# A linear-attention and two-MoE kernel: block transposes by DMA in SBUF, zeros in seven parts, routing over four products

## Chip, cores, metric

One core of one Trainium2 chip. The metric is the device time of one execution in microseconds (us), the median of the runs shown.

## What is computed

Three layers in a row, all float32. Cut from the reference:

```python
# attention: batch 8, heads 8, seq 576, head_dim 64
kv  = einsum('bhsd,bhse->bhde', k, v)
out = einsum('bhsd,bhde->bhse', q, kv)
x   = out / sqrt(mean(out*out, -1) + 1e-6) * g_norm      # -> [4608 tokens, 512]
# first MoE layer, dense: d_ff 768
h = maximum(maximum(x @ w1, x @ w2), x @ w3)
x = h @ w_out
# second MoE layer: 8 experts, the best 2 of each token, d_ff 1024
noisy = x @ w_gate + log1p(exp(x @ w_noise)) * noise
out[mask] += top2_w * (maximum(x[mask] @ w1[e], 0) @ w2[e])
```

Each float32 operand of the large products is held as a high and a low part (`hi`, `lo`), and a product is three passes over these: hi*hi, hi*lo, lo*hi.

## The kernel before

The 4,608 tokens are cut into nine chunks of 512 (0 to 8). The program has two halves: the chunks run through attention, the first MoE layer and routing (up to about 702 us), and then units of 128 to 512 tokens run through the experts. Every engine has one queue that it works off in order; the order is that in which the Python program writes the instructions. In chunk 0 a small planner, `run_tasks`, sets that order; the change leaves it alone.

**One chunk c.** The loop at the end of `body` writes for g = 0 to 17 first `misc1(c, g)` and then `g1(c, g)`, and after the 18 products `window(c)`. A product `g1` (line 311 for the matmuls) is 12 matmuls of 128x512 into one of four `hbank` PSUM banks; `g1_top` (lines 327 and 329, "top") takes it to `hm`, on ScalarE for every third product and on VectorE for the others, and after each third product `hsplit` (lines 315 and 319) writes a slice f of `hT` as hi and lo. Chunk 1 is shorter: half of its tokens were done in chunk 0, so its products have 256 columns.

**The window.** `g2(c, i, f0, f1)` (line 357) multiplies the six slices of `hT` of 128 tokens, block i, with `w_out`: 36 matmuls into two of the four `abank` banks. When a block is complete, lines 360 to 365 copy it out, half on VectorE and half on ScalarE, to `RA`. The last slice, f = 5, comes out of product 17.

**Attention for chunk c+1 runs inside chunk c.** At g = 10 `kv_pair` (line 192) and `kv_out` make the key-value product. `ao` (line 214) is 64 small matmuls for half the chunk; `norm` squares them (ScalarE, line 231), sums (VectorE, line 235), makes the inverse root with a few small instructions (lines 239 to 247) and scales (VectorE, line 251) into four buffers `xn`, one per block of 512 columns. Half 0 of `ao` stands at g = 14, half 1 in the window after block 1. Then `xtrans` turns the result for the next chunk's products: four transposes by TensorE into a PSUM bank (line 273), ScalarE writes `xT` hi (line 277) and VectorE lo (line 282). Four `xtrans` per window: two after block 1, two inside block 3. Product 0 of chunk c+1 reads all of `xT`.

**Loads.** SyncE's queue (SP) loads for each chunk the noise (16 KB), q into `RB`, and k, v into `KV0` and two buffers of `STG`; these stand at g = 0 and start when their buffers come free. At g = 11 of chunk 8 it starts the first expert weights (line 144), and then `load_rows` (line 755), a DMA that transposes 16-bit planes from HBM.

**Routing of chunk c-1 runs inside chunk c**: `route_a` (lines 385 to 408) as one block at g = 1, with two loads of the function table of ScalarE; `route_b` at g = 10 (7 in chunk 1), then four row scatters on GpSimd (POOL, line 427), and four more at g = 14 (12 in chunk 1).

**Zeros.** The output is added to later, so it is zeroed first: `zero_out`, one DMA of 9,472 KB from POOL's queue at g = 2 of chunk 2 (line 540).

Of the kernel before, what the change touches and what calls it, by code (L numbers as in the profile page):

```python
# [22 lines left out]
DUMMY = NE * R  # L23
# [62 lines left out]
def body(tc, A, dbg=None):  # L86
# [37 lines left out]
    def hbank():  # L124
        cnt["h"] += 1
        return HB[(cnt["h"] - 1) % 4]

    def abank():
        cnt["a"] += 1
        return AC[(cnt["a"] - 1) % 4]  # L130
# [72 lines left out]
    def ao(c, j, banks):  # L203
        for h in range(2):
            ao_bank[c, 2 * j + h] = banks[h]
        for i in range(2):
            t0 = (2 * j + i) * 128
            for p in range(4):
                o = slice(i * 256 + p * 64, i * 256 + (p + 1) * 64)
                for x in range(2):  # L210
                    t = t0 + x * 64
                    kb = KB[(c * CT + t) // S % 2]
                    for h in range(2):
                        PE.matmul(banks[h][HALF[x], o], qv(c)[HALF[h], p, t:t + 64],  # L214
                                  kb[HALF[h], p * 64:(p + 1) * 64], start=True, stop=True)
# [39 lines left out]
    def norm(c, i, x=None):  # L255
        norm_a(c, i, x)
        norm_b1(c, i, i + 1)
        norm_b2(c, i, i + 1)
        norm_c(c, i)
# [25 lines left out]
    def xtrans(c, i):  # L285
        t = xtrans_pe(c, i)
        xtrans_hi(i, t)
        xtrans_lo(i, t)


    def split(src, w):
        ACT.activation(w[:, 0:1024], src, AF.Copy)  # L292
        DVE.tensor_tensor(w[:, 1024:2048], src, w[:, 0:1024].bitcast(F), op=OP.subtract)  # L293
# [54 lines left out]
    def g2(c, i, f0, f1):  # L348
        if f0 == 0:
            x2b[i] = abank(), abank()  # L350
        s = slice(i * 128, (i + 1) * 128)
        for f in range(f0, f1):
            h = hTf(f)
            w = wo(f // 2)[:, :, f % 2]
            for n, (a, b) in enumerate(((0, 0), (0, 1), (1, 0))):
                for z, (lo, hi) in enumerate(((0, 256), (256, 528))):
                    PE.matmul(x2b[i][z][:, 0:hi - lo], h[:, a, s], w[:, b, lo:hi],  # L357
                              start=f == 0 and n == 0, stop=f == 5 and n == 2)
        if f1 == 6:
            DVE.tensor_copy(lgs[:, i, :], x2b[i][1][:, 256:272])  # L360
            for z in range(2):
                b = x2b[i][z].bitcast(U16).rearrange("p (n t) -> p n t", t=2)
                for q in range(2):
                    (ACT.copy if q else DVE.tensor_copy)(  # L364
                        planes[:, i, q * 512 + z * 256:q * 512 + z * 256 + 256], b[:, 0:256, q])
# [18 lines left out]
    def route_a(c):  # L384
        ACT.activation(nl, lgs[:, :, 8:16], AF.Exp)
        ACT.preload_act_table_set("natural_log")
        ACT.activation(nl, nl, AF.Ln, bias=1.0)
        ACT.preload_act_table_set(LNEXP)
        DVE.tensor_tensor(nl, nl, noise[c % 2], op=OP.mult)
        DVE.tensor_tensor(nl, nl, lgs[:, :, 0:8], op=OP.add)  # L390
        for i in range(4):
            DVE.max(m8[:, i, :], nl[:, i, :])
            DVE.max_index(ix[:, i, :], m8[:, i, :], nl[:, i, :])
        DVE.tensor_copy(ixf, ix[:, :, 0:2])
        for k in range(2):
            DVE.tensor_tensor(oh[:, k], C("iota8").unsqueeze(1).to_broadcast([128, 4, 8]),
                              ixf[:, :, k:k + 1].to_broadcast([128, 4, 8]), op=OP.is_equal)
        DVE.tensor_tensor(Mb, oh[:, 0], oh[:, 1], op=OP.add)
        DVE.tensor_copy(Cb[:, 1, :], Mb[:, 0, :])
        for i in range(1, 4):  # L400
            DVE.tensor_tensor(Cb[:, i + 1, :], Cb[:, i, :], Mb[:, i, :], op=OP.add)
        DVE.tensor_tensor(wt[:, 0, :], m8[:, :, 1], m8[:, :, 0], op=OP.subtract)
        ACT.activation(wt[:, 1, :], wt[:, 0, :], AF.Exp)
        DVE.tensor_scalar(wt[:, 0, :], wt[:, 1, :], 1.0, 1e-9, op0=OP.add, op1=OP.add)
        DVE.reciprocal(wt[:, 0, :], wt[:, 0, :])
        DVE.tensor_tensor(wt[:, 2, :], wt[:, 1, :], wt[:, 0, :], op=OP.mult)
        DVE.tensor_copy(rows[:, :, 512], wt[:, 0, :])
        DVE.tensor_copy(rows[:, :, 513], C("tok", 4 * c, 4 * c + 4))
# [24 lines left out]
    def scatter(c, k):  # L433
        if k == 1:
            DVE.tensor_copy(rows[:, :, 512], wt[:, 2, :])
        for i in range(4):
            scatter_to(si[c % 2][:, 4 * k + i:4 * k + i + 1], rows[:, i, :])
# [98 lines left out]
        POOL.memset(pad, 0.0)  # L536
        DVE.tensor_copy(pad[:, 513:514], C("trash"))

    def zero_out():
        z = POOL.dma_start(A["out"].rearrange("(a p) f -> p a f", p=128),  # L540
                           pad[:, 0:512].unsqueeze(1).to_broadcast([128, OUT_ROWS // 128, 512]))
        zeroed.append(z.ins)
        POOL.dma_start(Xg[DUMMY:DUMMY + 512, :].rearrange("(a p) w -> p a w", p=128),
                       pad.bitcast(U16).unsqueeze(1).to_broadcast([128, 4, 2 * XW]))

    for j in range(2):
        ao(0, j, [abank(), abank()])
# [279 lines left out]
            state["load"] += 1  # L827


    def misc1(c, g):  # L830
        if c == 1 and g == 0:
            POOL.memset(STG[2][64:128, 0:1024], 0.0)
            fills()
        if c == 1 and (g == 0 or 8 < g < 14):
            f = max(g - 8, 0)
            hsplit(f, early(f), 0, 256)
        if c == 2 and g == 2:
            zero_out()
        if g == 0:
            SP.dma_start(noise[c % 2], A["noise"][c])  # L840
        if g == 0 and 0 < c < NCH - 1:
            load_q(c + 1)
            if c + 1 < NB:
                for i in range(3):
                    load_kv(c + 1, i)
        if c > 0:
            if g == 1:
                route_a(c - 1)
            if g == (7 if c == 1 else 10):
                route_b(c - 1)  # L850
                scatter(c - 1, 0)
            if g == (12 if c == 1 else 14):
                scatter(c - 1, 1)
        if 0 < c < NB - 1 and g == 10:
            bank = abank()
            for p in range(4):
                kv_pair(c + 1, p, bank)
            kv_out(c + 1, bank)
        if 0 < c < NCH - 1 and g == 14:
            ao(c + 1, 0, [abank(), abank()])  # L860
            for i in range(2):
                norm(c + 1, i)
        if c == NCH - 1:
            if g == 11:
                spec_pick()
                load_regs(0, spi[0:1, 0:1], spi[0:1, 1:2])
                regE[1] = regE[0]
                regS[1] = SP.value_load(spi[0:1, 2:3], min_val=0, max_val=DUMMY)
                for p in range(3):
                    load_pair(p)  # L870
            if g == 12:
                load_rows(0)
            if g in (13, 14, 15, 16, 17):
                splits(1)

    def window(c):
        nx = c + 1 < NCH

        def fill(i):
            if nx:  # L880
                if i == 0:
                    ao(c + 1, 1, [hbank(), hbank()])
                norm(c + 1, i + 2)

        def trans(i):
            xtrans(c + 1, i)

        if c == 0:
            for i in (2, 3):
                g2(0, i, 0, 3)  # L890
                trans(i)
                g2(0, i, 3, 6)
            xn_n[0] = 0
            return
        for i in range(4):
            g2(c, i, 0, 3)
            if nx and i == 3:
                trans(2)
                trans(3)
            g2(c, i, 3, 6)  # L900
            if nx and i == 1:
                trans(0)
                trans(1)
                fill(0)
                fill(1)
            if not nx:
                if i < 2:
                    for r in range(3 * i, 3 * i + 3 - i):
                        utrans(0, r, 4)
                if i == 1:  # L910
                    load_rows(1)
                splits(1)
# [241 lines left out]
            G2(*fifo.pop(0)[1:])  # L1154

    def table():
        route_a(c)
        yield
        route_b(c)
        scatter(c, 0)  # L1160
        pads()
        yield
        yield from tab_counts()
        yield
        for n, _ in enumerate(tab_build()):
            if n == 2:
                scatter(c, 1)
            yield
        yield
        tab_out()  # L1170
        yield
        for uu in range(2, 4):
            regs_of(uu)
        load_rows(2)
        loads()
# [85 lines left out]
```

## Time and profile before

| | |
|---|---|
| median of 3 runs | 1540.65 us (1538.05 to 1541.68) |
| the profiled execution | 1540.13 us |
| its span, first to last instruction | 1538.4 us |
| TensorE busy | 1508.5 us (98%), mean granted clock 0.994 |
| VectorE, ScalarE, POOL busy | 789.7 us (51%), 644.8 us (42%), 222.3 us (14%) |
| chunks | 1 to 8 begin at about 143.1, 195.6, 269.4, 343.1, 416.9, 490.7, 564.4 and 635.6 us |

Durations below come from the profiled execution. "Busy" counts an instruction from its start to its modelled end; matmuls overlap their neighbours, so the price of a group on TensorE is the distance between starts, not the busy time. In the views by line and in the timelines, a bracket or a last column says how long the engine stood idle before an instruction and which instruction released it. In the views by stretch the last three numbers are the granted TensorE clock, the busy share of the 16 DMA engines and the GB/s that they moved. "To landing" is the time from the issue of a DMA until its data has arrived.

### The profile page before, as it was taken

How to read it: one execution, taken by the hardware profiler on the slowest of the kernel's cores; microseconds unless marked ns; L12 is line 12 of the kernel's file. 1: busy time of each engine (PE TensorE's matmuls, PEld its weight loads, DVE VectorE, ACT ScalarE, POOL GpSimd, SP SyncE). 2: the span in 40 equal slices, each digit the busy share in tenths (PEclk: the TensorE clock that was granted, in tenths of full speed). 3: DMA queues.
4: the chain of work that ended last, by engine and by line, in shares of the span. 5: the costliest groups of instructions: out<-in, count | busy, mean ns of one | idle time of the engine just before them, and what ended most of it. 6: DMA issues, size and time to landing. Idle time of an engine off the chain costs nothing.

```text
span 1538.4 us, 23747 instructions
## 1 busy us (share of the span) xinstructions
PE 1508.5 (98%) x9564; PEld 1304.2 (85%) x9564; DVE 789.7 (51%) x1567; ACT 644.8 (42%) x1042; POOL 222.3 (14%) x326
## 2 busy tenths in 40 slices
PE   5999999999999999999999999999999999999997
PEld 4789989898989898988888888888888888888886
DVE  5985534343435353447454465565364554545543
ACT  3554222222313131335254455556465454645543
POOL 0000211111110202023311102102011011211112
PEclk8999999999999999999999999999999999999999
DMA  8322652030303101063685578778486674957654
GB/s 296 137 83 91 235 220 117 30 117 29 118 36 112 54 32 56 1 192 98 192 208 135 140 210 193 191 225 213 135 210 147 181 196 133 227 128 211 157 151 78
DMA packets 132292, 219.82 MB, mean 143 GB/s; under 512 B 96464, under 2 KB 96720, under 8 KB 114640
## 3 DMA queue, kind: packets, MB, share of 16 engines
q1 hardware_dynamic: 112320, 166.50, 34.2%
q0 software_dynamic: 19856, 51.73, 14.9%
q8 instruction: 77, 1.26, 0.3%
q14 instruction: 39, 0.32, 0.1%
HBM read 146.30 MB, written 51.72 MB: 129 GB/s over the span
## 4 chain that ended last, share of the span: by engine, by line
PE 96%; DMA 1%; DVE 1%; ACT 1%; issue 0%; POOL 0%; SPq 0%; POOLq 0%; DVEq 0%; ACTq 0%
PE bank L311 28%; PE bank L1136 27%; PE bank L1074 26%; PE bank L357 10%; PE bank L192 1%; PE bank L1088 1%; PE bank L214 1%; PE bank L273 1%; DMA pad<-kvr 1%; DMA G<-kv 0%; DMA G<-w1s 0%; PE bank L501 0%; DVE RA L478 0%; DVE B L282 0%; PE bank L493 0%
## 5 line engine op out<-in xcount | busy, mean ns | idle before, releaser
L311 PE MATMUL bank<-B,W 128*128 128x512 f32 (+1 forms) x2160 | 455.4, 371 | 6.7 <-ACT W L482 4.1
L311 PEld LDWEIGHTS bank<-B,W 128*128 128x128 f32 x2160 | 377.4, 190 | 76.0 <-ACT W L482 4.9
L1136 PE MATMUL bank<-W,B 128*128 128x512 f32 x1728 | 421.3, 390 | 0.0
L1136 PEld LDWEIGHTS bank<-W,B 128*128 128x128 f32 x1728 | 320.2, 188 | 63.4
L1074 PE MATMUL bank<-B,W 128*128 128x512 f32 (+1 forms) x1728 | 353.0, 342 | 0.0
L1074 PEld LDWEIGHTS bank<-B,W 128*128 128x128 f32 x1728 | 280.5, 189 | 42.5
L293 DVE TENSOR_TENSOR W<-G,W 128x1024 fp32r<-128x1024 f32 x200 | 242.4, 1224 | 124.5 <-ACT W L292 124.1
L1078 ACT ACTIVATE B<-bank 128x512 fp32r<-128x512 f32 (+1 forms) x176 | 91.5, 520 | 340.8 <-PE bank L1074 340.8
L1079 DVE SCALAR_TENSOR_TENSOR B<-bank,B 128x512 fp32r<-128x512 f32 (+1 forms) x176 | 104.3, 593 | 238.9 <-ACT B L1078 237.9
L292 ACT ACTIVATE W<-G 128x1024 fp32r<-128x1024 f32 x200 | 208.4, 1053 | 39.3 <-PE bank L1136 24.8
L357 PE MATMUL bank<-W,B 128*128 128x256 f32 (+1 forms) x1296 | 163.9, 285 | 0.0
L357 PEld LDWEIGHTS bank<-W,B 128*128 128x128 f32 x1296 | 160.2, 188 | 1.1
L427 POOL DMA_INDIRECT Xg<-RA,si x72 | 72.5, 1007 | 519.4 <-issue 377.5
L329 DVE TENSOR_TENSOR hm<-hm,bank 128x512 f32<-128x512 f32 (+1 forms) x106 | 69.5, 655 | 132.5 <-PE bank L311 125.7
L315 ACT ACTIVATE B<-hm 128x512 fp32r<-128x512 f32 (+1 forms) x53 | 32.1, 606 | 184.2 <-DVE hm L329 184.2
L1074 PE MATMUL bank<-xlo,W 128*128 128x512 f32 x384 | 102.6, 389 | 0.0
L1110 POOL DMA_INDIRECT out<-xn,idt x37 | 61.6, 1664 | 271.6 <-ACT xn L1141 264.6
L1074 PEld LDWEIGHTS bank<-xlo,W 128*128 128x128 f32 x384 | 72.1, 188 | 15.0
L1110 POOL DMA_INDIRECT out<-x2T,idt x19 | 30.4, 1598 | 260.3 <-ACT x2T L1141 257.9
L364 ACT COPY RA<-bank 128x256 uint16<-128x256 uint16 x72 | 25.7, 373 | 87.9 <-DVE RA L364 72.6
L327 ACT ACTIVATE hm<-bank 128x512 f32<-128x512 f32 (+1 forms) x53 | 30.4, 573 | 53.8 <-PE bank L311 41.5
L1110 POOL DMA_INDIRECT out<-hm,idt x19 | 33.0, 1735 | 134.2 <-ACT hm L1141 130.4
(184 smaller groups left out, 1029.7 us busy)
## 6 DMA issues: line engine op xcount, KB each, us to landing
G<-mw SPq DMA_DIRECT2D x100, 1024.0 KB, 5.2
G<-w1s SPq DMA_DIRECT2D x12, 1024.0 KB, 5.1
out<-pad POOLq DMA_DIRECT2D x1, 9472.0 KB
kv<-kv SPq DMA_DIRECT2D x8, 1024.0 KB, 8.0
G<-kv SPq DMA_DIRECT2D x8, 1024.0 KB, 10.0
RB<-qT SPq DMA_DIRECT2D x8, 1024.0 KB, 4.9
G<-kvr SPq DMA_DIRECT2D x7, 256.0 KB, 10.8
Xg<-RA,si POOLq DMA_INDIRECT x72, 2.8
```

The costliest lines, as they stand in the source:

```text
L292: ACT.activation(w[:, 0:1024], src, AF.Copy)
L293: DVE.tensor_tensor(w[:, 1024:2048], src, w[:, 0:1024].bitcast(F), op=OP.subtract)
L311: PE.matmul(bank[:, 0:t1 - t0], w_in(g)[:, a, k, s], x[b][:, k, t0:t1], start=n == 0 and k == 0, stop=n == 2 and k == 3)
L315: ACT.activation(hTf(f)[:, 0, t0:t1], hm, AF.Copy)
L329: DVE.tensor_tensor(hm, hm, bank, op=OP.max)
L357: PE.matmul(x2b[i][z][:, 0:hi - lo], h[:, a, s], w[:, b, lo:hi], start=f == 0 and n == 0, stop=f == 5 and n == 2)
L427: i = POOL.indirect_dma_start(out=Xg, out_offset=bass.IndirectOffsetOnAxis(ap=idx, axis=0), in_=src, in_offset=None)
L1074: PE.matmul(bank[:, 0:n], w[:, a, k, s], x[b][:, k, 0:n], start=z == 0, stop=z == 11)
L1078: ACT.activation(h[:, 0, 0:n], bank[:, 0:n], AF.Relu)
L1079: DVE.scalar_tensor_tensor(h[:, 1, 0:n], bank[:, 0:n], 0.0, h[:, 0, 0:n].bitcast(F), op0=OP.max, op1=OP.subtract)
L1110: d = POOL.indirect_dma_start(out=A["out"], out_offset=bass.IndirectOffsetOnAxis(ap=idt[u % 3][:, i:i + 1], axis=0), in_=y, in_offset=None ...
L1136: PE.matmul(obank[i], h[:, a, s], w[:, b, ff % 2, :], start=ff == 0 and n == 0, stop=ff == 7 and n == 2)
```

## The change

- **Attention (chunks 2 to 8).** Both halves of `ao` stand at g = 12, squares and sums at g = 12 and 13, the inverse roots of all four blocks together at g = 13, the scaling at g = 14 and 15. `planes_out` copies each scaled block as two 16-bit planes (one copy on VectorE, one on ScalarE) into `KV0`; `planes_turn` is one DMA transpose on SP's queue for each two blocks, from `KV0` to `RB`, 128 x 2048 elements of 16 bits (512 KB). In the window, after blocks 0 and 1, `planes_in` merges the planes of two blocks each in an `STG` buffer (again one copy on each engine) and writes `xT` hi and lo from there. TensorE's transposes of these chunks are gone; those of chunks 0 and 1 stay. The blocks of `g2` stand one behind the other.
- **Zeros.** Seven DMAs of 1,280 or 1,536 KB, one at g = 10 of each of chunks 2 to 8, behind the first four scatters.
- **Routing.** `route_a` becomes a generator with three stops; its pieces stand at g = 1, 2, 3 and 4.

```diff
+    def xplanes(c):
+        return [t.bitcast(U16)[:, 0:4096] for t in (KV0, RB)]
+
+    def planes_out(c, b):
+        d = xplanes(c)[0].rearrange("p (b z k i e) -> p b z i k e", b=4, z=2, k=2, i=2)
+        x = xn_of[c, b].bitcast(U16).rearrange("p (i k e z) -> p z i k e", i=2, k=2, z=2)
+        for z in range(2):
+            (ACT.copy if z else DVE.tensor_copy)(d[:, b, z], x[:, z])
+
+    def planes_turn(c, j):
+        src, dst = xplanes(c)
+        SP.dma_start_transpose(out=dst[:, j * 2048:(j + 1) * 2048].rearrange("p (q t) -> p q t", q=16),
+                               in_=src[:, j * 2048:(j + 1) * 2048])
+
+    def planes_in(c, b):
+        p = xplanes(c)[1].rearrange("p (b z n) -> p b z n", b=4, z=2)
+        m = STG[c % 2][:, b * 512:(b + 1) * 512]
+        h = m.bitcast(U16).rearrange("p (n z) -> p n z", z=2)
+        for z in range(2):
+            (ACT.copy if z else DVE.tensor_copy)(h[:, :, z], p[:, b, z])
+        j, k = divmod(b, 2)
+        m = m.rearrange("p (k t) -> p k t", k=2)
+        hi, lo = (x[:, 2 * k:2 * k + 2, j * 256:j * 256 + 256] for x in xT)
+        ACT.activation(hi, m, AF.Copy, scale=gn[:, 0:1])
+        DVE.scalar_tensor_tensor(lo, m, gn[:, 0:1], hi.bitcast(F), op0=OP.mult, op1=OP.subtract)
+
+    def attend(c, n):
+        if n == 0:
+            for j in range(2):
+                ao(c, j, [abank(), abank()])
+        if n < 2:
+            for b in (2 * n, 2 * n + 1):
+                norm_a(c, b)
+        if n == 1:
+            norm_b1(c, 0, 4)
+            norm_b2(c, 0, 4)
+        if n in (2, 3):
+            j = n - 2
+            for b in (2 * j, 2 * j + 1):
+                norm_c(c, b)
+                planes_out(c, b)
+            planes_turn(c, j)
...
-    def zero_out():
-        z = POOL.dma_start(A["out"].rearrange("(a p) f -> p a f", p=128),
-                           pad[:, 0:512].unsqueeze(1).to_broadcast([128, OUT_ROWS // 128, 512]))
+    ZB = [0, 6, 12, 17, 22, 27, 32, 37]
+
+    def zero_out(n):
+        a, b = ZB[n], ZB[n + 1]
+        z = POOL.dma_start(A["out"][a * 128:b * 128, :].rearrange("(a p) f -> p a f", p=128),
+                           pad[:, 0:512].unsqueeze(1).to_broadcast([128, b - a, 512]))
...
-        if c == 2 and g == 2:
-            zero_out()
...
-                route_a(c - 1)
+                ra[c] = route_a(c - 1)
+            if 0 < g < 5:
+                next(ra[c], None)
             if g == (7 if c == 1 else 10):
                 route_b(c - 1)
                 scatter(c - 1, 0)
+                if c > 1:
+                    zero_out(c - 2)
...
-        if 0 < c < NCH - 1 and g == 14:
-            ao(c + 1, 0, [abank(), abank()])
-            for i in range(2):
-                norm(c + 1, i)
+        if 0 < c < NCH - 1 and g >= 12:
+            attend(c + 1, g - 12)
...
         for i in range(4):
-            g2(c, i, 0, 3)
-            if nx and i == 3:
-                trans(2)
-                trans(3)
-            g2(c, i, 3, 6)
-            if nx and i == 1:
-                trans(0)
-                trans(1)
-                fill(0)
-                fill(1)
-            if not nx:
-                if i < 2:
+            g2(c, i, 0, 6)
+            if i < 2:
+                if nx:
+                    for b in (2 * i, 2 * i + 1):
+                        planes_in(c + 1, b)
```

**Where instructions move.** SP's queue between the loads that stand in chunk 1 and those of chunk 2, as a piece of the difference (kv is `KV0`, G an `STG` buffer):

```order
 L163 DMA G_84<-kvr 64x1024
-L840 DMA noise_101<-noise 128x32
+L302 DMA_TRANSPOSE RB<-kv_92 128x16x128 x2
+L890 DMA noise_101<-noise 128x32
 L172 DMA RB<-qT 128x2048
 L155 DMA kv_92<-kv 128x2048
```

The two transposes stand ahead of the next chunk's noise, q and key-value loads; they read the buffer that the key-value load fills and write the one that the q load fills.

VectorE's queue before, in chunk 1, from the scaling of block 0 to the tops of products 16 and 17 (`xn` the scaled blocks, `stat` the sums, line 329 a top, line 319 a low half of `hT`):

```order
L251 TENSOR_TENSOR xn_93<-bank_111,stat 128x512
L235 TENSOR_REDUCE stat<-xn_94 128x8
L239 TENSOR_SCALAR stat<-stat 128x8
L245 TENSOR_TENSOR stat<-stat 128x8
L246 SCALAR_TENSOR_TENSOR stat<-stat 128x8
L247 SCALAR_TENSOR_TENSOR stat<-stat 128x8
L251 TENSOR_TENSOR xn_94<-bank_112,stat 128x512
L329 TENSOR_TENSOR hm_96<-hm_96,bank_105 128x256
L319 TENSOR_TENSOR B_87<-hm_96,B_87 128x256
L329 TENSOR_TENSOR hm_96<-hm_96,bank_107 128x256
L329 TENSOR_TENSOR hm_96<-hm_96,bank_108 128x256
```

The same place in the changed kernel, from the top of product 13 to that of product 16 (line 372 is the top, line 362 the low half of `hT`, line 298 `planes_out`):

```order
L372 TENSOR_TENSOR hm_96<-hm_96,bank_108 128x256
L251 TENSOR_TENSOR xn_93<-bank_111,stat 128x512
L298 COPY kv_92<-xn_93 128x2x2x128
L251 TENSOR_TENSOR xn_94<-bank_112,stat 128x512
L298 COPY kv_92<-xn_94 128x2x2x128
L372 TENSOR_TENSOR hm_96<-hm_96,bank_105 128x256
L362 TENSOR_TENSOR B_87<-hm_96,B_87 128x256
L251 TENSOR_TENSOR xn_95<-bank_109,stat 128x512
L298 COPY kv_92<-xn_95 128x2x2x128
L251 TENSOR_TENSOR x2T_97<-bank_110,stat 128x512
L298 COPY kv_92<-x2T_97 128x2x2x128
L372 TENSOR_TENSOR hm_96<-hm_96,bank_107 128x256
```

Before, blocks 0 and 1 stand ahead of the tops of products 14, 16 and 17 and blocks 2 and 3 in the window; now all four blocks, with a copy of each, stand between the tops of products 13 and 16, ahead of the last slice of `hT`.

## Rows read from the trace of the kernel before

**Rows 1.** The page, parts 1 (busy us, share, instructions) and 4 (chain)

```profile
PE 1508.5 (98%) x9564; PEld 1304.2 (85%) x9564; DVE 789.7 (51%) x1567; ACT 644.8 (42%) x1042; POOL 222.3 (14%) x326
...
PE 96%; DMA 1%; DVE 1%; ACT 1%; issue 0%; POOL 0%; SPq 0%; POOLq 0%; DVEq 0%; ACTq 0%
```

**Rows 2.** Waits of TensorE, whole span: us in total, times, longest us

```profile
PE bank L311 <- DVE hm L329: 1.4, 1, 1.4
```

**Rows 3.** Busy time by stretch: the windows of chunks 1, 7 and 8

```profile
core 0: us, PE busy (x) PEld busy (x) DVE busy (x) ACT busy (x) POOL busy (x), PEclk, DMA share, GB/s
174.72:195.42 20.70, 20.70 (x226) 20.37 (x225) 11.81 (x32) 7.51 (x19) 0.81 (x2) 1.00 1.02 391
...
614.70:635.40 20.70, 20.70 (x225) 20.35 (x224) 10.31 (x27) 6.93 (x17) 0.00 (x0) 1.00 0.01 2
684.55:702.11 17.56, 17.56 (x145) 17.56 (x144) 11.69 (x25) 8.77 (x16) 0.64 (x2) 1.00 0.53 155
```

**Rows 4.** Timeline of TensorE, chunk 2's window: start us, us, what, count

```profile
248.49 8.95 PE L357 MATMUL bank<-W,B 128*128 128x256 f32 x72
257.28 1.03 PE L273 MATMUL bank<-cst,xn 128*128 128x128 f32 x8
258.24 1.16 PE L214 MATMUL bank<-kvt,RB 64*64 64x64 f32 x64
259.33 6.87 PE L357 MATMUL bank<-W,B 128*128 128x256 f32 x54
266.04 0.38 PE L273 MATMUL bank<-cst,xn 128*128 128x128 f32 x2
...
266.91 2.44 PE L357 MATMUL bank<-W,B 128*128 128x256 f32 x18
269.19 3.13 PE L311 MATMUL bank<-B,W 128*128 128x512 f32 x13
```

**Rows 5.** Chain that ended last, products 0 to 9 of chunk 2: start us, us

```profile
195.58 27.22 PE bank L311 x120
```

**Rows 6.** Groups of VectorE, 195 to 700 us: busy us, mean ns, idle before

```profile
L329 DVE TENSOR_TENSOR hm<-hm,bank 128x512 f32<-128x512 f32 x84 | 57.6, 686 | 125.4 <-PE bank L311 120.0 <-ACT hm L327 4.3 <-DVE hm L329 0.5
...
L251 DVE TENSOR_TENSOR xn<-bank,stat 128x512 f32<-128x512 f32 x18 | 12.4, 692 | 1.9
L235 DVE TENSOR_REDUCE stat<-xn 128x8 f32<-128x512 f32 x18 | 12.2, 678 | 5.4 <-ACT xn L231 5.4
```

**Rows 7.** Groups of ScalarE, same stretch

```profile
L315 ACT ACTIVATE B<-hm 128x512 fp32r<-128x512 f32 x42 | 26.5, 632 | 171.4 <-DVE hm L329 171.4
...
L231 ACT ACTIVATE xn<-bank 128x512 f32<-128x512 f32 x18 | 10.7, 597 | 19.4 <-PE bank L214 19.4
```

**Rows 8.** Instructions of line 788: duration ns min/median/max

```profile
L788 DVE COPY mg<-RB x59: 441/452/573, 689.9 to 1512.6; 128x512 uint16<-128x512 uint16 x59
L788 ACT COPY mg<-RB x47: 762/771/788, 690.3 to 1511.2; 128x512 uint16<-128x512 uint16 x47
```

**Rows 9.** Line 755, DMA transposes from HBM

```profile
DMA to landing us min/median/max: 4.2/5.6/16.0
```

**Rows 10.** DMA issues, 698 to 704 us: KB each, us to landing

```profile
RB<-Xg SPq DMA_TRANSPOSE x1, 5.9
```

**Rows 11.** Timeline of TensorE, chunk 1, product 5

```profile
151.82 3.13 PE L311 MATMUL bank<-B,W 128*128 128x256 f32 x24 [1.38 <-DVE hm L329]
```

**Rows 12.** Timeline of VectorE, chunk 1, tops of half width

```profile
151.35 0.94 DVE L329 TENSOR_TENSOR hm<-hm,bank 128x256 f32<-128x256 f32 x2
```

**Rows 13.** Timeline of ScalarE, chunk 8, products 14 to 17 and window

```profile
675.23 2.01 ACT L292 ACTIVATE W<-G 128x1024 fp32r<-128x1024 f32 x2 [3.49 <-DMA G<-mw]
...
686.62 0.63 ACT L315 ACTIVATE B<-hm 128x512 fp32r<-128x512 f32 x1 [2.68 <-DVE hm L329]
```

**Rows 14.** Timeline of SP's queue, chunk 8, product 11

```profile
670.24 1.50 SPq L144 DMA_DIRECT2D G<-mw  x3
```

**Rows 15.** Busy time by stretch while the zeros go out

```profile
177.00:193.00 16.00, 16.00 (x187) 15.67 (x186) 8.87 (x26) 5.33 (x15) 0.00 (x0) 1.00 1.02 385
```

More of the change, by code (lines that the diff above doesn't have):

```diff
@@ L390, in route_a @@
         DVE.tensor_tensor(nl, nl, lgs[:, :, 0:8], op=OP.add)
+        yield
         for i in range(4):
@@ L393, in route_a @@
             DVE.max_index(ix[:, i, :], m8[:, i, :], nl[:, i, :])
+        yield
         DVE.tensor_copy(ixf, ix[:, :, 0:2])
@@ L401, in route_a @@
             DVE.tensor_tensor(Cb[:, i + 1, :], Cb[:, i, :], Mb[:, i, :], op=OP.add)
+        yield
         DVE.tensor_tensor(wt[:, 0, :], m8[:, :, 1], m8[:, :, 0], op=OP.subtract)
@@ L537, in fills @@
         DVE.tensor_copy(pad[:, 513:514], C("trash"))
-    def zero_out():
-        z = POOL.dma_start(A["out"].rearrange("(a p) f -> p a f", p=128),
-                           pad[:, 0:512].unsqueeze(1).to_broadcast([128, OUT_ROWS // 128, 512]))
+    ZB = [0, 6, 12, 17, 22, 27, 32, 37]
[3 more added lines that the diff above has]
+                           pad[:, 0:512].unsqueeze(1).to_broadcast([128, b - a, 512]))
         zeroed.append(z.ins)
-        POOL.dma_start(Xg[DUMMY:DUMMY + 512, :].rearrange("(a p) w -> p a w", p=128),
-                       pad.bitcast(U16).unsqueeze(1).to_broadcast([128, 4, 2 * XW]))
+        if n == 0:
+            POOL.dma_start(Xg[DUMMY:DUMMY + 512, :].rearrange("(a p) w -> p a w", p=128),
+                           pad.bitcast(U16).unsqueeze(1).to_broadcast([128, 4, 2 * XW]))
     for j in range(2):
@@ L827, in loads @@
             state["load"] += 1
+    ra = {}
     def misc1(c, g):
@@ L877, in window @@
         nx = c + 1 < NCH
[L879 to L886, printed above, removed]
         if c == 0:
@@ L890, in window @@
                 g2(0, i, 0, 3)
-                trans(i)
+                xtrans(1, i)
                 g2(0, i, 3, 6)
@@ L895, in window @@
         for i in range(4):
-            g2(c, i, 0, 3)
-            if nx and i == 3:
-                trans(2)
-                trans(3)
-            g2(c, i, 3, 6)
-            if nx and i == 1:
-                trans(0)
-                trans(1)
-                fill(0)
-                fill(1)
-            if not nx:
-                if i < 2:
+            g2(c, i, 0, 6)
[3 more added lines that the diff above has]
+                        planes_in(c + 1, b)
+                else:
                     for r in range(3 * i, 3 * i + 3 - i):
                         utrans(0, r, 4)
+            if not nx:
                 if i == 1:
@@ L1156, in table @@
     def table():
-        route_a(c)
+        for _ in route_a(c):
+            pass
         yield
```

## The prediction

> **What bounds the kernel.** I read the page first: TensorE is busy 98% of the span and holds 96% of the chain that ended last [rows 1]. A kernel of this kind gets shorter only where work leaves TensorE's queue or where TensorE waits. Then its waits: from chunk 1 on there is one, 1.4 us for a top on VectorE [rows 2]; it stands ahead of products 5 and 6 of chunk 1 [rows 11]. Everything else on VectorE, ScalarE, POOL and the DMA queues is hidden today. So the questions are what leaves TensorE's queue, and what comes out from under its cover.
>
> **What leaves TensorE.** The window of chunk 8 shows a window without attention: 144 matmuls in 17.56 us, 4.39 us a block. The windows of chunks 1 to 7 take 20.70 us, the first as the seventh [rows 3]. In these stand 16 transposes and one half of `ao`. The half of `ao` moves to g = 12 and is paid there: it goes from 258.24 to 259.33, 1.09 us [rows 4]. What is left is 20.70 - 17.56 - 1.09 = 2.05 us a window. The transposes alone, from start to start, are 258.24 - 257.28 = 0.96 and 266.91 - 266.04 = 0.87, together 1.83 us [rows 4]; the other 0.2 us is spent around the switches between transposes and matmuls. Seven windows: 7 x 2.05 = **14.3 us**, at least 7 x 1.83 = 12.8. I take 14.3, since the changed window is that of chunk 8, back to back.
>
> **The routing.** In chunk 1 the whole of `route_a` stands ahead of the top of product 1 on VectorE, and product 5 needs that bank. Now only its first piece does; the others come after later tops, and the half-width tops are short, 0.94 us for two [rows 12]. The wait of 1.38 us [rows 11] goes: **-1.4 us**, between 0 (the third and fourth piece hold up product 8 as long) and 1.4. In later chunks products take 27.22 / 10 = 2.72 us [rows 5] and no wait is there to be saved.
>
> **What VectorE and ScalarE take on.** Each block now passes two more copies on each engine. Such a 16-bit copy of 128x512 takes 0.45 us on VectorE and 0.77 on ScalarE [rows 8]; eight a chunk are 3.6 and 6.2 us, against a cover of some 74 us a chunk (269.4 - 195.6), and over the span these engines are busy 51% and 42% [rows 1]. Only two places are tight. In chunks 2 to 7: with `ao` at time 0, product 12 starts at 2 x 1.09 = 2.2, the window at 2.2 + 6 x 2.72 = 18.5, and its blocks end every 4.39 us, the last at 36.1. Product 13 ends at 7.6; its top (0.69), two scalings at 0.69, two copies at 0.45 on VectorE and the last copy on ScalarE (0.77) [rows 6, 8] put the first DMA transpose at about 12, the second, behind the top and split of product 14, at about 16.5. The last slice of `hT` follows product 17 as before. No wait.
>
> In **chunk 1** the products are half as long. From the first square (0.60 us [rows 7], done at 1.09 + 0.60 = 1.7) VectorE has four sums (0.68), four scalings (0.69), four copies (0.45), some 1.2 us of small instructions and eight half-width ones (0.47) [rows 6, 8, 12]: 12.2 us, some 1.3 more in waits for ScalarE, so the last slice of `hT` comes at about 15. The six products last 6 x 1.48 = 8.9 (3.13 us for two [rows 11], less the overlap), so the window begins at 11.1 and asks for slice 5 after 30 matmuls of 4.39 / 36, at 14.8. I charge **+0.5 us**, between 0 and 1.6.
>
> **The DMA transposes.** No row shows one within SBUF. The nearest are those from HBM of 1 MB, twice the bytes: 5.9 us to landing with the queues nearly empty [rows 10], 4.2 the shortest of all and 16.0 the longest, which was beside weights [rows 9]. A half-size one costs between 2.1 (half the shortest) and 16.0; I take 5, near the lone one. Who waits: `planes_in` reads the first after block 0 of the window and its copy-out, at about 24, the second at about 28.3, 12 us after each issue; and product 0 of the next chunk needs `xT` at 36.1, while the two blocks behind 28.3 take about 4 us (copy 0.77, high part 0.63, low part 0.69 as for like shapes [rows 6 to 8], twice). If each takes X and the second queues behind the first, all is ready at 12 + 2X + 4, in time for X up to 10 us. So 5 is hidden, and half of the slowest row (8) is too: **0 us**. Behind these DMAs in SP's queue stand the noise, q and key-value loads of the next chunk but one; they wait for the buffers `RB` and `KV0`, free about 4 us ahead of the window's end, and are asked for at g = 10 or later, 27 us into the next chunk: 0.
>
> The Trainium skill speaks against this step: its page "VectorE: DVE Perf Modes", section "The three transpose paths", gives 1309 ns for one 128x128 transpose by DMA against 390 on TensorE, and the rules below it prefer TensorE where PSUM will do as the target. By that figure, as an estimate, 16 of them one after the other would be 21 us, past the 10 above. Against it speaks the trace's lone megabyte, 32 such squares in 5.9 us [rows 10].
>
> **The zeros.** The one large DMA moved 385 GB/s and kept the DMA engines full [rows 15], and TensorE did not wait; in chunks 2 to 7 nothing is won or lost. The seventh part is new at a bad place. In chunk 8 it goes out just ahead of the first expert weights (SP issues them at 670.24 [rows 14]), 1,280 KB at 385 GB/s, 3.4 us. ScalarE there already idles 3.49 us for these weights [rows 13], its queue carries the splits of the weights and the last slice of `hT`: 686.62 + 0.63 = 687.25 for its high part, which block 0 asks for at 684.55 + 30 x 0.122 = 688.2. So only 1 us of slack; weights late by 1 to 3.4 us cost 0 to 2.5. Both queues share the engines, so I take 2 late, **+0.9 us**.
>
> **The sum** against the profiled execution's own 1540.13 us (span 1538.4 and 1.73 around it; the median of the runs is 0.5 above): 1540.1 - 14.3 - 1.4 + 0.5 + 0.9 = **1525.8 us**, 0.9% faster. A measurement of this kernel tells about 0.2%, 3.1 us, from no change.
>
> **Rivals.**
> - *VectorE and the weights come out from under the cover.* Chunk 1 pays 1.6, chunk 8 pays 2.5, the routing saves nothing and a window saves only 1.83: 1540.1 - 12.8 + 1.6 + 2.5 = 1531.4. For it speaks the small slack at both places; against it that all four at once are needed.
> - *The DMA transposes come late: slower.* Place: product 0 of each of chunks 2 to 8 waits for `xT`. Price: 2 us a chunk for each us of X above 10, so 14 us in all. At X = 11 the gain is used up; at 12 the time is 1525.8 + 28 = 1554, at the 16.0 of the slowest row 1525.8 + 84 = 1610. For it: a source in SBUF is unpriced, and the scatters of g = 14 share the DMA engines. Against it: the lone row, at half of which X is 3.
> - *The 16 squares of one DMA transpose go one after the other*, so that X is beyond the slowest row and the time over 1610. Against it: no row of a transpose is that slow. The figure of the Trainium skill's page named above would make this X = 21.
> - *Nothing changes for TensorE*: the windows keep their length because the 0.2 us and the transposes were filling time in which the tops were awaited. Then 1540. Against it: the window of chunk 8, with more on VectorE (11.69 us against 10.31), is short [rows 3].
>
> **Chances.** The forecast, 1524 to 1529: 0.74. First rival, 1529 to 1534: 0.13. DMA transposes late: 0.08, of which 0.02 still faster, 0.02 within 0.2% and 0.04 slower. One square after the other: 0.03, slower. No effect: 0.02, the same. So faster 0.89, same 0.04, slower 0.07. The range 1523.8 to 1533.5 goes from all costs at zero (1540.1 - 14.3 - 1.4 = 1524.4, less a little) over the first rival, and leaves out late transposes.
>
> **What would show it.** Right: windows of 17.6 us in chunks 1 to 7, TensorE's chain without line 273 after chunk 1, no wait ahead of product 5 of chunk 1, DMA transposes landing in 4 to 8 us. Wrong: waits of product 0 for VectorE's `xT` behind `planes_in`, or of block 0 of the windows of chunks 1 and 8 for ScalarE's half of slice 5, over 2 us.

## The result and the profile after

| | before | changed |
|---|---|---|
| median | 1539.97 us (4 runs, 1538.05 to 1541.68) | 1526.62 us (4 runs, 1525.79 to 1527.96) |
| the profiled execution | 1540.13 us | 1526.44 us |
| its span | 1538.4 us | 1524.7 us |

The ratio is 0.9912, with a 95% interval of 0.9897 to 0.9927: 13.4 us less, where the forecast was 1525.8 us. The page of the changed kernel, with busy time (parts as in [rows 1]), the chain, and TensorE's group of the window (line 400 is `g2` there; its last column is the idle time before it):

```profile
PE 1495.7 (98%) x9452; PEld 1294.1 (85%) x9452; DVE 796.4 (52%) x1539; ACT 675.5 (44%) x1056; POOL 229.0 (15%) x332
...
PE 95%; DMA 2%; ACT 1%; DVE 1%; issue 0%; POOL 0%; SPq 0%; POOLq 0%; DVEq 0%
...
L400 PE MATMUL bank<-W,B 128*128 128x256 f32 (+1 forms) x1296 | 162.1, 286 | 2.1 <-ACT B L358 2.1
```

TensorE has 112 matmuls and 12.8 us of work less; VectorE has 6.7 us more, ScalarE 30.7. In the last row is something new: 2.1 us in which TensorE waits for line 358, the high part of a slice of `hT`. The timeline of TensorE, for chunk 1, chunk 2 and the end of chunk 8:

```profile
142.61 10.22 PE L354 MATMUL bank<-B,W 128*128 128x256 f32 x84
...
191.10 27.37 PE L354 MATMUL bank<-B,W 128*128 128x512 f32 x120
...
226.61 2.10 PE L214 MATMUL bank<-kvt,RB 64*64 64x64 f32 x128
228.64 16.62 PE L354 MATMUL bank<-B,W 128*128 128x512 f32 x72
...
666.96 3.82 PE L400 MATMUL bank<-W,B 128*128 128x256 f32 x30
672.84 15.70 PE L400 MATMUL bank<-W,B 128*128 128x256 f32 x114 [2.06 <-ACT B L358]
688.37 6.98 PE L1111 MATMUL bank<-B,W 128*128 128x512 f32 x30
```

The first row is products 0 to 6 of chunk 1 without a gap, so the wait of [rows 11] is gone. In chunk 2 both halves of `ao` stand together and take 2.03 us (226.61 to 228.64); no row of line 273 is left there. In chunk 8 the new wait of 2.06 us stands at slice 5 of block 0. Busy time by stretch: the windows of chunks 1 and 7 (against 20.70 in [rows 3]), and three stretches behind the wait of chunk 8:

```profile
173.53:191.10 17.57, 17.57 (x146) 17.57 (x145) 10.78 (x26) 9.91 (x19) 0.00 (x0) 1.00 0.36 88
600.27:617.84 17.57, 17.57 (x146) 17.56 (x144) 8.22 (x19) 8.40 (x15) 0.00 (x0) 1.00 0.07 15
...
672.84:676.00 3.16, 3.16 (x14) 3.16 (x15) 2.07 (x6) 0.87 (x3) 0.00 (x0) 0.51 1.05 393
676.00:677.00 1.00, 1.00 (x9) 1.00 (x8) 0.23 (x1) 1.00 (x2) 0.00 (x0) 0.85 0.70 295
677.00:690.00 13.00, 13.00 (x103) 12.71 (x102) 8.44 (x17) 7.89 (x14) 0.00 (x0) 1.00 0.40 85
```

The windows are as short as that of chunk 8 before. Behind the wait the granted clock (third number from the end) is 0.51, its lower level of 1.2 GHz, for some 3 us, and then 1.00 again: 14 matmuls in 3.16 us, where 26 would go at full clock. The window of chunk 8 lasts 688.37 - 666.96 = 21.41 us in place of 17.56: 2.06 of wait and 1.8 at the lower clock.

**The account**, span against span, in us: a chunk lasts 262.66 - 191.10 = 71.56 (the window of chunk 2 is 245.09 to 262.66) and lasted 73.77, and 7 x 2.2 = **-15.4**; the wait in chunk 1 **-1.4**; chunk 8 **+3.8**; chunk 1 began 0.5 earlier, which is in chunk 0, where nothing was changed (over the thirteen profiled executions used here its start scatters between 142.2 and 145.7 us, though no edit touches chunk 0); 0.2 is left over. Together -13.7, from 1538.4 to 1524.7.

Why chunk 8 waits is read on two queues. POOL and SP there, issues with their time (line 589 is a zeros part, line 144 the first expert weights), from the two timelines:

```profile
651.84 0.92 POOL L589 DMA_DIRECT2D out<-pad  x1
...
652.71 2.18 SPq L144 DMA_DIRECT2D G<-mw  x3
```

The same place on ScalarE (line 335 splits weights, line 358 is the high part of the last slice):

```profile
660.76 2.01 ACT L335 ACTIVATE W<-G 128x1024 fp32r<-128x1024 f32 x2 [6.61 <-DMA G<-mw]
...
672.15 0.63 ACT L358 ACTIVATE B<-hm 128x512 fp32r<-128x512 f32 x1 [2.67 <-DVE hm L372]
```

The part is issued 0.87 us ahead of the weights, and ScalarE waits 6.61 us for these, against 3.49 in [rows 13]. Its queue then runs 3.1 us later up to the last slice, which TensorE wants. So the step is the predicted one, and its price four times the predicted one.

The transposes themselves, the 14 of line 302, with the time to landing of the 11 whose landing the trace has:

```profile
L302 SPq DMA_TRANSPOSE RB<-kv x14: 1317/1676/4445, 173.7 to 598.0; - x14
...
DMA to landing us min/median/max: 3.7/3.8/7.9
```

No engine waited for one.

### The profile page after: what moved, and what is told of

Read it like the earlier page. It is cut to its first block, busy times and chain, and to the rows that moved or that the text cites. A ratio compares the mean times of both kernels' runs of the same rounds, so it can differ in the third digit from the quotient of the medians.

```text
span 1524.7 us, 23555 instructions
## 1 busy us (share of the span) xinstructions
PE 1495.7 (98%) x9452; PEld 1294.1 (85%) x9452; DVE 796.4 (52%) x1539; ACT 675.5 (44%) x1056; POOL 229.0 (15%) x332
## 4 chain that ended last, share of the span: by engine, by line
PE 95%; DMA 2%; ACT 1%; DVE 1%; issue 0%; POOL 0%; SPq 0%; POOLq 0%; DVEq 0%
PE bank L354 28%; PE bank L1173 27%; PE bank L1111 26%; PE bank L400 10%; PE bank L192 1%; PE bank L1125 1%; PE bank L214 1%; DMA pad<-kvr 1%; DMA G<-mw 1%; DMA G<-kv 0%; PE bank L547 0%; DVE hm L372 0%; ACT B L277 0%; PE bank L539 0%; ACT W L335 0%
```

## The experiments

The theory after the result: the transposes by DMA save 2.2 us a chunk and are hidden; the routing saves its wait; the seventh zeros part alone costs 3 to 5 us in chunk 8. The rivals: the wait in chunk 8 has another cause; the saving is something else than the transposes; the transposes are close to coming late.

The runs were made on three chips of different speed. The kernel before took 1547.5 us on the chip of the first run of six parts and of the routing, the zeros and the transposes alone; 1547.6 us on that of the changed kernel again, six parts again and the repeated transposes; and 1540.7 us on that of the small and large last part and the one zeros DMA earlier. So each run is compared with the kernel before, or with another kernel, on its own chip.

### Six zeros parts, none in chunk 8

```diff
-    ZB = [0, 6, 12, 17, 22, 27, 32, 37]
+    ZB = [0, 7, 13, 19, 25, 31, 37]
...
-                if c > 1:
+                if 1 < c < NCH - 1:
                     zero_out(c - 2)
```

> The changed kernel with the zeros in six parts, in chunks 2 to 7, none in chunk 8. Theory (the part in chunk 8 makes the first expert weights late, and with them the last slice of hT): TensorE's wait of 2.06 us in block 0 of chunk 8's window goes, the granted clock stays at 1.00 there, chunk 8 shrinks from 70.5 us back to about 66.7, and the time falls by about 3.8 us, to 1522.8 us. Rival (the weights are late for another reason, since everything before them now comes earlier): the wait stays at 2 us and the time at 1526.6 us.

Measured: 1528.86 us, ratio to the kernel before 0.988 (0.9864 to 0.9897). Its timelines of TensorE and of ScalarE in chunk 8:

```profile
671.32 17.72 PE L400 MATMUL bank<-W,B 128*128 128x256 f32 x144
688.88 8.33 PE L1111 MATMUL bank<-B,W 128*128 128x512 f32 x36
```

```profile
662.18 2.01 ACT L335 ACTIVATE W<-G 128x1024 fp32r<-128x1024 f32 x2 [3.66 <-DMA G<-mw]
```

The window is 17.56 us in one piece, and ScalarE's wait for the weights is back at 3.66 us. The wait in chunk 8 was the seventh part's.

### The changed kernel again, beside six parts

The six-part kernel and the changed one, unedited, five rounds each on one chip.

> The changed kernel as it is, timed beside the next one on the same chip. Theory: as the first time, ratio to before 0.991 (on a chip whose own time before is higher, a little lower), with a wait of about 2 us in block 0 of chunk 8's window; whether the granted clock falls behind that wait is open: behind 2.06 us it fell to 0.5, behind 2.44 us in the kernel with the zeros alone it stayed at 1.00. Rival: the wait is there only in the execution that was profiled first, and the six-part version beside it has the same time.

> The version with the zeros in six parts and none in chunk 8, once more, beside the changed kernel. Theory: 2 to 3.8 us less than the changed kernel on the same chip, no wait in chunk 8. Rival: the same time.

Measured: the changed kernel 1533.04 us, ratio 0.9907 (0.989 to 0.9923); six parts 1528.57 us, ratio 0.9881 (0.9865 to 0.9898): 4.5 us between the medians, where 2 to 3.8 had been expected. Of the 4.6 us between the two profiled spans (1530.8 and 1526.2), 2.0 lie ahead of chunk 1's window (it begins at 178.06 and at 176.06), in chunk 0, where both run the same rows; 2.9 are the window of chunk 8, and 0.3 is won back behind it. The window in the timeline of the changed kernel, and the stretch behind its wait:

```profile
672.90 3.82 PE L400 MATMUL bank<-W,B 128*128 128x256 f32 x30
678.87 14.61 PE L400 MATMUL bank<-W,B 128*128 128x256 f32 x114 [2.15 <-ACT B L358]
693.32 8.33 PE L1111 MATMUL bank<-B,W 128*128 128x512 f32 x36
```

```profile
678.87:682.00 3.13, 3.13 (x23) 2.94 (x24) 1.96 (x6) 1.17 (x3) 0.00 (x0) 1.00 1.05 389
```

The wait is there again, but this time the granted clock stayed at 1.00 behind it. The window lasts 693.32 - 672.90 = 20.42 us, 2.9 more than 17.56: 2.15 of wait and 0.7 that the granted clock doesn't account for. So the seventh part cost 2.9 us here and 3.8 where the clock fell.

### A small and a large last part

```diff
-    ZB = [0, 6, 12, 17, 22, 27, 32, 37]
+    ZB = [0, 6, 12, 18, 24, 30, 35, 37]
```

(512 KB; the large one, 2,048 KB, has `[0, 5, 10, 15, 20, 25, 29, 37]`.)

> The changed kernel with the seventh zeros part cut to 512 KB (the sixth parts grow). Theory (chunk 8 loses what the last part takes of the DMA engines ahead of the first expert weights): ScalarE waits 4 to 5 us for G<-mw there, TensorE waits 0 to 0.5 us in chunk 8, and the time is 1528 to 1530.5 on this chip. Rival (the part costs by being issued in chunk 8 at all, whatever its size): TensorE still waits about 2 us, time about 1533.

> The changed kernel with the seventh zeros part grown to 2,048 KB (1,280 before). Theory: 768 KB more at some 385 GB/s is 2 us more, so ScalarE waits 8 to 9 us for G<-mw, TensorE 3.5 to 4.5 us in chunk 8, time 1534.5 to 1538 on this chip. Rival (a fixed price): wait about 2 us, time about 1533.

Measured, one execution each, on a chip where the kernel before took 1540.7 us (the expected times were for 1547.5): 1523.24 us small, 1534.57 us large. Against the kernel before that is 17.5 us less with the small part, as expected (17 to 19.5), and 6.1 less with the large one, where 9.5 to 13 had been expected; the changed kernel itself wasn't run on this chip. TensorE's window of chunk 8, first with the small part, then with the large one:

```profile
667.63 18.19 PE L400 MATMUL bank<-W,B 128*128 128x256 f32 x144
685.66 4.71 PE L1111 MATMUL bank<-B,W 128*128 128x512 f32 x20
```

```profile
670.01 3.82 PE L400 MATMUL bank<-W,B 128*128 128x256 f32 x30
676.48 11.53 PE L400 MATMUL bank<-W,B 128*128 128x256 f32 x78 [2.65 <-ACT B L358]
690.11 6.40 PE L400 MATMUL bank<-W,B 128*128 128x256 f32 x36 [2.10 <-ACT RA L407]
696.35 3.82 PE L1111 MATMUL bank<-B,W 128*128 128x512 f32 x16
```

The window lasts 18.0 us with 512 KB, 21.4 with 1,280 KB and 26.3 with 2,048 KB: 0.5, 3.8 and 8.8 us above 17.56. Of the last, 4.75 are waits, a little more than expected, and behind both of them the granted clock is down to 0.50 again. ScalarE waits 4.50 us for the weights with the small part, as expected, and 6.02 and then 1.86 us with the large one, 7.9 together in place of 8 to 9. The price goes with the size, and the rival of a fixed price for a part in chunk 8 falls. Of the 11.3 us between the two times, 2.4 arose ahead of chunk 1's window (174.19 and 176.59) and 8.3 in chunk 8.

### The routing alone

The kernel before, with `route_a` as a generator in four places and nothing else.

```diff
-                route_a(c - 1)
+                ra[c] = route_a(c - 1)
+            if 0 < g < 5:
+                next(ra[c], None)
```

> The kernel before with only the routing spread over four products. Theory: the wait of 1.38 us ahead of product 5 of chunk 1 goes and nothing takes its place, 1538.6 us. Rival: a later piece holds up product 6, 7 or 8 of chunk 1 as long, the sum of TensorE's waits stays, 1540.0 us.

Measured: 1548.18 us, ratio 0.9997 (0.9987 to 1.0006). Timeline of TensorE, chunk 1:

```profile
143.88 10.22 PE L311 MATMUL bank<-B,W 128*128 128x256 f32 x84
```

The wait is gone as in the changed kernel, so the spread routing is what removes it. In the total, 1.4 us (0.09%) is too little to be seen.

### The zeros alone

The kernel before, with the seven zeros parts of the changed kernel and nothing else.

```diff
-        if c == 2 and g == 2:
-            zero_out()
...
+                if c > 1:
+                    zero_out(c - 2)
```

> The kernel before with only the zeros in seven parts. Theory: the part in chunk 8 costs what it costs in the changed kernel, a wait of 2 us for the last slice of hT and some 1.7 us at a granted clock of about 0.5 behind it: 1543.8 us, and nothing in chunks 1 to 7. Rival (the seventh part only hurts together with the transposes): 1540.0 us.

Measured: 1551.4 us, ratio 1.0029 (1.0018 to 1.0039). Timeline of TensorE, chunk 8:

```profile
697.45 14.41 PE L357 MATMUL bank<-W,B 128*128 128x256 f32 x114 [2.44 <-ACT B L315]
```

Alone this edit loses 3.9 us against the 1547.5 of the kernel before, 2.44 of it this wait (behind which the granted clock of the profiled run stayed at 1.00). The window of chunk 8 lasts 20.51 us, 2.9 more than the 17.57 of the kernel with the routing alone on this chip; where the last 1.0 us went isn't shown. The total is as expected (3.8), but the part of it that was put down to the clock did not show. By this run the parts are a pure cost. The next one shows what they are needed for.

### The transposes alone

The changed kernel with `route_a` in one block and the zeros in one DMA, as in the kernel before.

```diff
-                if c > 1:
-                    zero_out(c - 2)
...
+        if c == 2 and g == 2:
+            zero_out()
```

> The changed kernel with the routing in one block and the zeros in one DMA as before. Theory: windows of 17.6 us, 2.2 us less in each of seven chunks, no wait in chunk 8: -15.4 us. But the one DMA of zeros runs at about 172 to 197 us and the two transposes for chunk 2 fall into it: they land in 8 us or more each in place of 3.8, and if the second lands after about 186 us product 0 of chunk 2 waits, up to some 8 us. So 1524.6 us where they come in time, up to 1533 us where not. Rival (the zeros don't slow the transposes, as the queues share the engines): 1524.6 us with the transposes of chunk 2 landing in 4 us like the others.

Measured: 1551.93 us, ratio 1.0032 (1.0019 to 1.0044). That is 4.5 us more than the kernel before on this chip. The theory had named the collision, but at some 8 us at most, and so expected a gain. Timeline of TensorE in chunk 1's window, then line 302 (its landings, and who waited for it):

```profile
180.64 13.47 PE L400 MATMUL bank<-W,B 128*128 128x256 f32 x108
214.40 6.32 PE L400 MATMUL bank<-W,B 128*128 128x256 f32 x36 [20.29 <-ACT RA L407]
```

```profile
L302 SPq DMA_TRANSPOSE RB<-kv x14: 1317/2456/14203, 181.4 to 628.7; - x14
...
  ACT G L310: 21.1, 1
...
DMA to landing us min/median/max: 3.7/4.5/27.7
```

The two transposes of chunk 2, issued from 181.40, are held up: they keep SP's queue for 27.5 us, and the first lands after 27.7 (the trace has no landing for the second). POOL's queue had issued the 9,472 KB of zeros at 175.51. While both are out, and behind the wait, the stretches show:

```profile
185.00:202.00 17.00, 9.11 (x75) 8.89 (x73) 2.02 (x6) 1.16 (x4) 0.00 (x0) 0.87 1.04 404
...
214.40:216.00 1.60, 1.60 (x6) 1.55 (x7) 0.19 (x1) 1.57 (x3) 0.00 (x0) 0.50 0.00 0
```

The DMA engines are full at 404 GB/s. `planes_in` on ScalarE (line 310) waits 21.1 us for `RB`; behind it in the queue stands line 407, the copy-out of a `g2` block; TensorE needs that bank, waits 20.29 us and goes on at half clock. 20.29, 1.05 and 1.38 for tops, and some 1.8 at the lower clock make 24.5, against 1551.93 - 1528.86 = 23.1 us from the six-part kernel on this chip. So the parts of this change don't add: the zeros in parts lose 3.9 us by themselves, and they are what keeps the transposes' 15.4.

### The transposes, with the one zeros DMA earlier

The last kernel again, with one number changed, so that the large DMA is out before the transposes are issued.

```diff
-        if c == 2 and g == 2:
+        if c == 1 and g == 2:
             zero_out()
```

> The transposes alone, with all zeros in one DMA of 9,472 KB as in the kernel before, but issued at product 2 of chunk 1 (about 127 us) and not at 175.5 us. Theory (the transposes alone lost only because this one DMA was in flight while chunk 2's two transposes were): the zeros are out at about 152 us, the transposes of chunk 2 land in 4 to 5 us, ScalarE does not wait for RB, the wait of 20.29 us is gone, and the time is 1529 to 1535 us on this chip (the six-part kernel's 1528.6, the routing's 1.4, and 0 to 5 for k, v and q of chunk 2, which are loaded beside the zeros from 143 us and are needed at 159). Rival (the transposes are slow by themselves when there is no zeros part, or the zeros must go in parts for another reason): a wait of 10 us or more stays in chunk 2's windows and the time is over 1540.

Measured: 1532.8 us, ratio 0.9953 (0.9937 to 0.997), beside 1540.7 us of the kernel before. That is 7.9 us less, where 12.5 to 18.5 less had been expected (1529 to 1535 against 1547.5). Its line 302, its timelines of TensorE, VectorE and POOL in chunk 1, and the large DMA among the issues of 115 to 260 us (KB, us to landing):

```profile
DMA to landing us min/median/max: 3.7/4.7/7.8
```

```profile
150.96 3.14 PE L354 MATMUL bank<-B,W 128*128 128x256 f32 x24 [1.38 <-DVE hm L372]
...
180.97 2.93 PE L354 MATMUL bank<-B,W 128*128 128x256 f32 x12 [5.17 <-DVE hm L372]
```

```profile
175.43 0.17 DVE L478 COPY RA<-wt 128x4 f32<-128x4 f32 x1 [7.52 <-DMA Xg<-RA,si]
```

```profile
166.60 1.04 POOL L470 DMA_INDIRECT Xg<-RA,si  x1 [22.04 <-DMA Xg<-pad]
```

```profile
out<-pad POOLq DMA_DIRECT2D x1, 9472.0 KB, 38.0
```

The point in dispute is settled: with the large DMA elsewhere the transposes land in 3.7 to 7.8 us (13 of the 14 landings are in the trace) and nobody waits for them, so it was the collision. But the new place has a price of its own. Beside the k, v and q loads the large DMA takes 38.0 us. `zero_out` also issues a second write, 1,040 KB into `Xg`, the target of the scatters, and the first scatter on POOL waits 22.04 us until that write has landed. VectorE waits 7.52 us for the scatters, and TensorE 5.17 us for a top behind that. So the loss here is not by shared DMA engines alone: the scatters wait for a write into their own buffer. In neither of the two places that were tried beside the transposes, in chunks 1 and 2, does the one large DMA go without a wait of TensorE; other places were not tried.

### Each transpose twice, and three times

On the six-part kernel, `planes_turn` issues its DMA 2 or 3 times, from and to the same buffers.

```diff
-        SP.dma_start_transpose(out=dst[:, j * 2048:(j + 1) * 2048].rearrange("p (q t) -> p q t", q=16),
-                               in_=src[:, j * 2048:(j + 1) * 2048])
+        for _ in range(2):
+            SP.dma_start_transpose(out=dst[:, j * 2048:(j + 1) * 2048].rearrange("p (q t) -> p q t", q=16),
+                                   in_=src[:, j * 2048:(j + 1) * 2048])
```

> The six-part version with each DMA transpose issued twice, one after the other (same bytes, same target), so that a half lands after about 7.7 us in place of 3.8. Theory (a half may take up to about 10 us in chunks 2 to 7): nothing changes there. In chunk 1, whose products are half as long, the second half lands about 3.4 us after planes_in would read it, and product 0 of chunk 2 waits some 2.3 us: 2 to 4 us more than the six-part version. Rival (the transposes are only just hidden): each of seven chunks waits 4 us or more, some 28 us more.

> The six-part version with each DMA transpose issued three times, so that a half lands after about 11.6 us. Theory (late by 2 x (11.6 - 10) = 3 to 4 us in chunks 2 to 7, by some 10 us in chunk 1): waits of product 0 of chunks 2 to 8 for xT, 28 to 34 us together, and up to 1.7 us more behind each where the granted clock falls: 30 to 46 us more than the six-part version. Rival (the slack is larger than worked out): under 10 us more.

Measured, one execution each: 1529.72 us with two, 1558.24 us with three, 1.2 and 29.7 above the six-part kernel (of the 1.2, 1.0 arose in chunk 0). The timeline of TensorE with two, the window of chunk 2, is unbroken; with three, behind the window of chunk 5, TensorE waits twice for line 315, which is the high part of `xT` in `planes_in` there:

```profile
249.35 17.72 PE L401 MATMUL bank<-W,B 128*128 128x256 f32 x144
266.91 18.31 PE L355 MATMUL bank<-B,W 128*128 128x512 f32 x80
```

```profile
480.11 17.73 PE L401 MATMUL bank<-W,B 128*128 128x256 f32 x144
499.98 0.73 PE L355 MATMUL bank<-B,W 128*128 128x512 f32 x2 [2.14 <-ACT B L315]
501.94 18.25 PE L355 MATMUL bank<-B,W 128*128 128x512 f32 x72 [1.23 <-ACT B L315]
```

With three, TensorE's waits for line 315 are 12.6 us in all, and one of 5.6 us is in chunk 1's window. The other 11.5 us go with a lower granted clock (its mean over the span is 0.988, with six parts 0.995). Two in a row cost less than expected. Three cost about the lower end of what was expected in all (30 to 46), but by other terms: the waits for `xT` had been put at 28 to 34. The slack of a half is thus more than one further landing of 3.7 us, and less than two.

## Why the prediction held, point by point

- **What bounds the kernel.** Right: TensorE held 95% of the chain after the change too, and what left its queue left the time.
- **The windows, -14.3.** Right in mechanism, 1.1 us short. The windows are 17.56 as forecast. The term took half of `ao` at 1.09 us a half, and both together take 2.03, not 2.18; so a chunk saves 2.2 us and not 2.05.
- **The routing, -1.4.** Right; the wait is gone in the changed kernel and with this part alone.
- **Chunk 1, +0.5.** Measured 0, and the step was misread. The last slice was forecast 3.9 us after the window's start and came later still, as the timeline of ScalarE in chunk 1's window (from 173.53) shows:

```profile
178.34 0.42 ACT L358 ACTIVATE B<-hm 128x256 fp32r<-128x256 f32 x1 [1.01 <-DVE hm L372]
```

  Its high part is done at 178.76, 5.2 us after the start, and yet no gap stands in the window. The prediction had block 0 ask for it after 30 matmuls. But the products of chunk 1 are only the 256 tokens of blocks 2 and 3; what blocks 0 and 1 read of `hT` comes from chunk 0 and was split by 167.7. Block 2 begins at 173.53 + 8.8 = 182.3 and asks for slice 5 after 30 matmuls, at 186.0, so the slack was 7.2 us and not 0.
- **The DMA transposes, 0.** Right: 3.8 us at the median where 5 was taken. The slack was put at X = 10 us for a half; two in a row cost nothing clear of the scatter, three in a row make X 11.9 (chunk 2: first issue 250.03, second half read at 273.85, 23.8 us for two) and cost 29.7 us, where "14 us for each us above 10" gives 26.6. That the totals are near is luck: product 0 of chunks 2 to 8 waited 12.6 us, less than half of that price, and the rest came from chunk 1's window and the lower clock. The rival of late transposes thus had its place right, its price for the waits too high and with no term for the clock, and its condition not met. The rival by which 16 squares go one after the other is refuted for this shape: 3.7 us for 16 squares are 0.23 us each. The figure of 1309 ns for one, in the Trainium skill's page "VectorE: DVE Perf Modes", section "The three transpose paths", is not what a square costs in a DMA of many.
- **The zeros, +0.9.** Right in place and chain, wrong in size: +3.8. The prediction had the weights late by 2 us, out of 1,280 KB at 385 GB/s, beside a slack of 1 us. They came 3.1 us later, near the 3.4 us of the whole part; TensorE waited 2.06 us, and then ran some 3 us at the lower clock, which cost 1.8 more, a term that the sum had not. The upper end given, 2.5, was too low for the same reason.
- **"In chunks 2 to 7 nothing is won or lost"** is true of the changed kernel and misses what the parts are for. No rival looked at the transposes beside the large DMA, because the change never lets them meet. Whoever had taken this change apart would have found two edits that each lose about 4 us alone.

The sum came out right to within 0.7 us of the profiled execution, and that closeness is luck, since errors cancel: 1.1 too little for the windows and 0.5 too much for chunk 1 stand against 2.9 too little for chunk 8, and 0.5 us came from chunk 0.

**A better version** follows from the one term that was mis-sized: six zeros parts, which end in chunk 7. It beats the kernel before by 1.2% (0.9881, 0.9865 to 0.9898) and the changed one by 4.5 us on the same chip, of which 2.0 in the profiled executions lie in chunk 0, outside the edit.

## What to carry to other kernels

Work that leaves the bounding engine for the DMA engines is worth what it was worth there, as long as its landing time fits the slack, and issuing it twice is a cheap way to measure that slack. A large DMA that nobody waits for still delays those beside it that somebody does wait for: cut it up, and put the pieces where only loads with slack are in flight, not just ahead of the first loads of the next stage. Parts of a change are to be priced together, since one that is a loss alone can be the condition of the gain.

## What was not expected of the hardware

- A DMA transpose of 512 KB within SBUF lands in 3.7 to 3.8 us at best and at the median, and took 27.7 us beside a 9,472 KB write, with the DMA engines full at 404 GB/s. It was issued 5.9 us behind that write.
- What a wait of TensorE costs can be much more than its length, but is not each time. Behind 2.06 us the granted clock fell to 0.51 for some 3 us; behind 2.15 us of the same wait in another run, and behind 2.44 us with the zeros alone, it stayed at 1.00, and the window lost only 0.5 to 0.7 us beside the wait. Behind 2.10, 2.65, 5.17 and 20.29 us it was at 0.50. What decides between the short ones isn't settled by these runs.
- Two of the three chips of the experiments were 0.5%, 7 us, slower with the kernel before. The traces of the runs on them show idle times of TensorE put down to "issue", for which no cause is seen: most of 0.35 to 0.45 us among the 64-column matmuls of lines 192 and 214, some of up to 1.1, together 2 to 4 us a run. The traces of the other runs don't have them. Where the rest of the 7 us goes isn't shown.
